# Attention scores made twice, by query and by key, in a kernel of attention and two expert layers

## The chip, the cores and the metric

The kernel runs on one core of a Trainium2 chip. The metric is the device time of one execution in microseconds (us), the median of several runs. The core has a matrix engine (TensorE, PE in the rows), a vector engine (VectorE, DVE), a scalar engine (ScalarE, ACT), GpSimd (POOL) and SyncE (SP), which issues most DMA transfers. Each engine executes its own instructions strictly in the order in which the program gave them, and waits at one whose inputs are not there.

## The reference

Cut to the first part, which the change touches; behind it stand a layer of 8 experts with balanced weights P and a two-layer network.

```python
B, H, S, D = 4, 8, 768, 64           # chunk 32, left 16, right 8, 8 memory keys
for c in range(S // 32):
    q_c = q[:, :, c_start:c_end]
    k_full = concat([mem_k, k[:, :, l_start:r_end]]); v_full = concat([mem_v, v[...]])
    scores = scale * q_c @ k_full.T
    scores = scores - max(scores)
    a = exp(scores)
    a = a / (sum(a) + 1e-9)
    out[:, :, c_start:c_end] = a @ v_full
# x: (3072, 512) -> experts: h = relu(x @ w1[e]); out += P[:, e] * (h @ w2[e]) -> relu(x @ w_in)**2 @ w_out
```

## The kernel before

Every matrix product works on pairs of fp16 numbers: a value is scaled by a power of two and split into a high part (ACT) and a low part (DVE: value minus high part), and a product is the sum of three or four products of parts.

Attention works on 32 tiles of 96 queries (three chunks) with all 8 heads, against 128 keys (16 left, 96, 8 right, 8 memory). A tile goes through `a_load` (q, k, v into a buffer `raw`), `a_scale` (maximum of q, k and v over each partition, L225, and a diagonal matrix of it, L157), `a_all` (a product with ones, L165, that brings the maxima of all partitions to each), `a_scale2` (L235 and the scale), `a_split` (high and low parts, two copies of k), `a_tqk` (q and k transposed by DMA, 24 blocks of 128 x 128), `a_scores` (a mask product L283 and 16 products L293; queries in partitions), `a_max` (L307, L309), `a_exp` (L316, 8 exponentials with the maximum as bias), `a_asplit` (high part L329, low part L330), `a_ta` (probabilities transposed by DMA, 16 blocks), `a_av` (24 products), `a_norm`, `a_xsplit` and `a_tx` (the output transposed into `xt`, 8 blocks).

Beside it runs the first expert on the tiles that are done: `gate`, `l1_pair` (24 products of 256 columns; relu on ACT, L698, low part on DVE, L699) and `l2_half` (12 products of 512 columns). Then come the balancing of the weights, the other experts and the last network, in which the change only renames banks of PSUM.

The order of the program is written out by hand. Each function gets a time on a made-up axis (`at(t, fn)`, in "units"), the list is sorted by that time and executed, so the times only set the order in which the instructions of each engine stand. Tile `i` starts at `ta(i)`, 10.957 units after the one before (`TA`); its steps lie at `OFF` behind it, for the first tiles between `TIGHT` and `OFF` (`when`). Blocks of the expert start when their tiles are done, stretched by `STR`. Steps of four or five tiles so alternate on each engine. [...]

Of the kernel before, what the change touches and what calls it, by code (L numbers as in the profile page):

```python
# [18 lines left out]
OFF = [-12.39, -1.44, 2.63, 7.14, 15.08, 26.35, 27.25, 30.29, 34.52, 41.29, 51.41, 52.02, 55.62, 62.46]  # L19
TIGHT = [-10.92, 0.2, 1.59, 2.57, 6.3, 11.37, 12.18, 16.3, 16.6, 18.11, 25.16, 25.81, 27.57, 29.09]  # L20
T0 = 5.78
TS = [6.0, 3.31, 5.8, 8.55, 10.0]
TA = 10.957
STR = 1.413
RAMP = 6.0
LDO = 4.245
SK = [0.01, 2.7, 2.52, 7.55, 7.55, 7.27, 6.55, 7.55, 7.55, 7.89, 7.55, 7.55, 5.95]
W_AT = [-4.79, 6.92, 8.93, 14.42, 18.96, 22.65, 33.67, 39.86, -4.25, 45.8, 3.81]
# [3 lines left out]
DN = [-0.34, 0.0, -0.45]  # L32
# [16 lines left out]
def tile_attention_moe_moe2(  # L49
# [14 lines left out]
    nc = tc.nc  # L64
# [23 lines left out]
    VP = 72  # L88
# [14 lines left out]
    ps = ctx.enter_context(tc.tile_pool(name="ps", bufs=3, space=bass.MemoryType.PSUM))  # L103
# [33 lines left out]
    onehot = ap_.tile([TQ, TQ], BF16, name="onehot")  # L137
    raws = [
# [83 lines left out]
    def a_scale(i):  # L222
        raw = raws[raw_of(i)]
        mx = sml.tile([P, 3], F32, tag="amx", name="amx")
        nc.vector.tensor_reduce(mx, raw, AX.X, ALU.max, apply_absolute_value=True)  # L225

        d = flat((lsb, pm)[i % 2]).bitcast(BF16).rearrange("p (n x) -> p n x", n=3)
        st[i, "dg"] = max_diag(mx, 3, d)

    def a_all(i):  # L230
        st[i, "gm"] = max_all(st.pop((i, "dg")), 3)

    def a_scale2(i):
        gm = sml.tile([P, 3], F32, tag="agm", name="agm")
        nc.vector.tensor_reduce(gm, st.pop((i, "gm")), AX.X, ALU.max)  # L235
# [13 lines left out]

    def a_split(i):  # L250
        raw = raws[raw_of(i)]
        sc = st.pop((i, "sc"))
        if i % 2 and i < LATE:
            qk = xt[NB - 1].rearrange("p s k n -> p (s k n)")[:, 0:6 * H * D]
            qk = qk.rearrange("p (a h s d) -> p a h s d", a=3, h=H, s=2)
        else:
            qk = ap_.tile([P, 3, H, 2, D], F16, tag="qk16", name="qk16")
        q16, k16 = qk[:, 0], qk[:, 1:3]
        v16 = v16s[i % NV]
        hd = lambda ap: ap.rearrange("p (h d) -> p h d", h=H)  # L260
        split(hd(raw[:, 1, :]), k16[:, 0, :, 0, :], k16[:, 0, :, 1, :], sc[:, 1:2])
        split(hd(raw[:, 0, :]), q16[:, :, 0, :], q16[:, :, 1, :], sc[:, 0:1])
        nc.vector.tensor_copy(k16[:, 1, :, 1, :], k16[:, 0, :, 0, :])
        nc.vector.tensor_copy(k16[:, 1, :, 0, :], k16[:, 0, :, 1, :])
        split(hd(raw[:, 2, :]), v16[:, 0, :, 0:D], v16[:, 1, :, 0:D], sc[:, 2:3])
        st[i, "qk"] = qk

    def a_tqk(i):
        qk = st.pop((i, "qk"))
        qkT = ap_.tile([P, 3, H, P], F16, tag="qkT", name="qkT", bufs=2)  # L270
        nc.sync.dma_start_transpose(
            out=qkT.rearrange("p a h n -> p (a h) n"), in_=qk.rearrange("p a h s d -> p (a h s d)")
        )
        st[i, "qkT"] = qkT

    def a_scores(i):
        qkT = st.pop((i, "qkT"))
        j = i % TPB
        mv = 0 if j == 0 else (2 if j == TPB - 1 else 1)
        scs = []  # L280
        for g in range(2):
            sc = psa.tile([TQ, 4, P], F32, tag="sc", name="sc", bufs=3)
# [3 lines left out]
                rhs=maskr[:, mv].unsqueeze(1).to_broadcast([TQ, 4, P]),  # L286
# [15 lines left out]

    def a_max(i):
        scs, sce = st[i, "scp"], st[i, "sce"]
        mx = sml.tile([TQ, 2, 4], F32, tag="smx", name="smx")
        for g in range(2):
            nc.vector.tensor_reduce(mx[:, g], scs[g], AX.X, ALU.max)  # L307
        nb = sml.tile([TQ, 2, 4], F32, tag="snb", name="snb")
        nc.vector.tensor_scalar(nb, mx, sce[0:TQ], -1.0, ALU.mult, ALU.mult)  # L309
        st[i, "nb"] = nb  # L310

    def a_exp(i):
        scs, sce, nb = st.pop((i, "scp")), st.pop((i, "sce")), st.pop((i, "nb"))
        e = ap_.tile([TQ, H, P], F32, tag="e", name="e")
        for h in range(H):
            nc.scalar.activation(  # L316
                e[:, h, :],
                scs[h // 4][:, h % 4, :],
                AF.Exp,
                scale=sce[0:TQ],  # L320
                bias=nb[:, h // 4, h % 4:h % 4 + 1],
            )
        st[i, "e"] = e

    def a_asplit(i):
# [1373 lines left out]
```

## Time and profile before

| | us |
|---|---|
| median of 3 runs (2658.33 to 2666.21) | 2661.05 |
| the profiled execution | 2665.82 |
| its span, first to last instruction | 2664.0 |
| busy in the span: PE, DVE, ACT, POOL | 2426.2, 1952.3, 1380.7, 1321.3 |

The span is cut in 40 slices of 66.6 us; the attention stage fills the first eight (the last transposition of its output is issued at 519.5 us). An idle engine costs time only where somebody waits for what it does next, so the views that name who waited for whom are read beside the busy times. Ends of matrix products are modelled in the trace: their starts are what can be relied on.

### The profile page before, as it was taken

Reading aid. Unit: us, or ns where it says so; the run is one execution under the profiler, and the core shown is the slowest. Engines: PE = TensorE matmul, PEld = TensorE weight load, DVE = VectorE, ACT = ScalarE, POOL = GpSimd, SP = SyncE. Lnnn points to the kernel's source line nnn. Section 1 sums busy time; section 2 is a strip of 40 time slices with the busy share of each in tenths; the row PEclk is TensorE's granted clock in tenths of the full one; section 3 lists DMA queues with packets and bytes.
Section 4 is the critical chain, followed back from the end, with each engine's and each line's share of the span. In section 5 each row is a group of like instructions: output and inputs, shape, how many; then the busy total and the mean of one; then the engine's idle time right before and its main releaser. Section 6 shows DMA issues by size and latency. Waiting matters only on the chain.

```text
span 2664.0 us, 51890 instructions
## 1 busy us (share of the span) xinstructions
PE 2426.2 (91%) x21138; PEld 2018.8 (76%) x21138; DVE 1952.3 (73%) x2844; ACT 1380.7 (52%) x2445; POOL 1321.3 (50%) x1105
## 2 busy tenths in 40 slices
PE   2578777989999999999999999999999989999998
PEld 1455545655667888888888888888888878888887
DVE  7778767476667887788787878877768897557555
ACT  4545544342334555556455555555556666666453
POOL 2211111153453566467366556655646776666343
PEclk9979978989999999999999999999999999999999
DMA  9799878423144435443534534353333365553221
GB/s 191 134 160 165 141 127 139 94 83 111 66 149 166 147 123 163 138 142 115 181 131 135 175 125 136 128 175 113 116 103 127 110 172 156 155 165 120 79 71 42
DMA packets 444471, 351.00 MB, mean 132 GB/s; under 512 B 323144, under 2 KB 377928, under 8 KB 437576
## 3 DMA queue, kind: packets, MB, share of 16 engines
q1 hardware_dynamic: 360614, 326.78, 43.3%
q10 hardware_dynamic: 83618, 20.91, 4.7%
q8 instruction: 165, 2.70, 0.4%
q14 instruction: 74, 0.61, 0.1%
HBM read 215.50 MB, written 77.07 MB: 110 GB/s over the span
## 4 chain that ended last, share of the span: by engine, by line
PE 62%; DVE 15%; POOL 4%; issue 3%; DMA 2%; ACT 2%; SPq 1%; ACTq 0%; DVEq 0%; POOLq 0%
PE pbA L822 28%; PE pbE L822 15%; PE pbB L822 7%; PE pb L822 3%; DVE xt L1020 2%; PE py L1178 2%; PE py L1180 2%; PE py L1179 2%; DVE acc L1133 1%; DVE hp L1020 1%; DVE wx L615 1%; DVE wb L615 1%; DMA w2d<-wst 1%; DVE amx L225 1%; DMA w2d<-tw 1%
## 5 line engine op out<-in xcount | busy, mean ns | idle before, releaser
L822 PEld LDWEIGHTS <-wb 128*128 128x128 f16 x5184 | 510.3, 99 | 68.4 <-DVE wb L615 4.2
L822 PEld LDWEIGHTS <-hp 128*128 128x128 f16 x4608 | 451.7, 98 | 61.8 <-issue 8.7
L822 PEld LDWEIGHTS <-wx 128*128 128x128 f16 x3888 | 380.3, 98 | 61.4 <-issue 17.6
L822 PEld LDWEIGHTS <-xt 128*128 128x128 f16 x3456 | 339.5, 99 | 81.9 <-DVE xt L1020 40.5
L822 PE MATMUL pbA<-w2p,hp 128*128 128x256 f16 x2304 | 290.7, 273 | 7.4 <-ACT xt L950 4.6
L822 PE MATMUL pbE<-xt,wx 128*128 128x256 f16 x2304 | 282.9, 273 | 14.6 <-DVE S L955 9.1
L822 PE MATMUL pbA<-S,wb 128*128 128x256 f16 x2304 | 287.4, 275 | 0.3 <-ACT S L950 0.3
L950 ACT ACTIVATE u<-pbA 128x512 f32<-128x512 f32 x181 | 107.4, 593 | 244.6 <-PE pbA L822 240.2
L330 POOL TENSOR_TENSOR a<-e,a 96x1024 f16<-96x1024 f32 x32 | 69.1, 2160 | 321.1 <-issue 204.9
L1178 PE MATMUL py<-w2p,hp 128*128 128x512 f16 x384 | 154.6, 403 | 9.4 <-DVE hp L699 5.5
L822 PE MATMUL pbA<-w2p,xt 128*128 128x256 f16 x1152 | 157.2, 273 | 0.0
L822 PE MATMUL pbE<-xt,xt 128*128 128x256 f16 x1140 | 155.5, 273 | 0.0
L822 PE MATMUL pbE<-xt,hp 128*128 128x256 f16 x1140 | 155.5, 273 | 0.0
L1179 PE MATMUL py<-w2p,hp 128*128 128x512 f16 x384 | 154.2, 401 | 0.0
L1180 PE MATMUL py<-w2p,hp 128*128 128x512 f16 x384 | 153.9, 401 | 0.0
L950 ACT ACTIVATE xt<-pbA 128x512 f32<-128x512 f32 x124 | 73.3, 592 | 140.6 <-PE pbA L822 136.0
L1020 POOL TENSOR_TENSOR hp<-u,hp 128x512 f16<-128x512 f32 x97 | 119.9, 1237 | 51.0 <-ACT hp L1013 50.3
L822 PE MATMUL pbA<-xt,wb 128*128 128x256 f16 x1152 | 142.5, 273 | 2.0 <-DVE wb L615 2.0
L822 PE MATMUL pbA<-S,wx 128*128 128x256 f16 x1152 | 141.5, 273 | 0.0
L822 PE MATMUL pbB<-xt,wb 128*128 128x256 f16 x1152 | 141.5, 273 | 0.0
L1020 DVE TENSOR_TENSOR hp<-xt,hp 128x512 f16<-128x512 f32 x80 | 88.9, 1111 | 62.1 <-ACT hp L1013 62.0
L950 ACT ACTIVATE S<-pbA 128x512 f32<-128x512 f32 x127 | 74.9, 591 | 114.2 <-PE pbA L822 112.2
(346 smaller groups left out, 5841.1 us busy)
## 6 DMA issues: line engine op xcount, KB each, us to landing
wst<-in_moe_w_dram SPq DMA_DIRECT2D x80, 512.0 KB
xt<-xdr SPq DMA_DIRECT2D x40, 1024.0 KB
S<-sdr SPq DMA_DIRECT2D x126, 256.0 KB
w2d<-wst SPq DMA_DIRECT2D x32, 512.0 KB
w2p<-w2d SPq DMA_DIRECT2D x32, 512.0 KB
wst<-in_moe_w_dram SPq DMA_DIRECT2D x56, 256.0 KB
xdr<-xt SPq DMA_DIRECT2D x12, 1024.0 KB
w2d<-tw SPq DMA_DIRECT2D x32, 384.0 KB
```

What stands on the lines that cost most here:

```text
L225: nc.vector.tensor_reduce(mx, raw, AX.X, ALU.max, apply_absolute_value=True)
L330: nc.gpsimd.tensor_tensor(al, e, ah, ALU.subtract)
L615: nc.vector.scalar_tensor_tensor(flat(d[:, 1]), f, scale(e, 0)[0], flat(d[:, 0]), ALU.mult, ALU.subtract)
L822: nc.tensor.matmul(p[:, r], lhsT=w[:, ws], rhs=x[:, xs], start=a, stop=z, skip_group_check=onto)
L950: nc.scalar.activation(t, p, AF.Copy, scale=sc)
L1020: eng.tensor_tensor(d[:, 1], t, d[:, 0], ALU.subtract)
L1133: nc.vector.scalar_tensor_tensor(a, z[:, tl], fc[:, t:t + 1], a, ALU.mult, ALU.add)
L1178: nc.tensor.matmul(p, lhsT=h[:, 1], rhs=w[:, 0], start=first, stop=False)
L1179: nc.tensor.matmul(p, lhsT=h[:, 0], rhs=w[:, 1], start=False, stop=False)
L1180: nc.tensor.matmul(p, lhsT=h[:, 0], rhs=w[:, 0], start=False, stop=last)
```

## The change

It replaces the transposition of the probabilities by a second computation of the scores. The first scores, queries in partitions, now serve the maximum alone. The maximum, split into a high and a low fp16 part (`a_max`), is transposed by a product with a unit matrix (`a_mt`, `a_mtc`); `a_st` computes the scores again with keys in partitions, and adds minus the maximum by 8 products with a constant matrix `minus` of 16 rows. So `a_exp` needs no bias per query, takes four heads in one instruction and gives probabilities that are already by key. Of the four products of parts of q and k, low times low is left out; the low parts lie in one half (64 rows) of the array, and q and k take 20 blocks of transposition.

`a_scale` no longer makes a diagonal matrix: a product with the unit matrix lays the maxima of 128 partitions in a row (`a_all`), DVE takes the row's maximum (`a_row_max`), and a product with ones spreads it (`a_spread`). High and low parts become steps of their own (`a_split`/`a_split_lo`, `a_xsplit`/`a_xsplit_lo`, `l1_pair`/`l1_lo`), a copy of q goes to POOL, and a table `STEPS` with new times replaces `OFF` and `TIGHT`; `TA` and `STR` stay. PSUM in the stage: 2 banks for `ps`, 1 for the short products, 3 for both kinds of scores, 2 for the values. `gate_prep` moves from 45.80 to 28.00 (`W_AT[9]`).

```diff
-OFF = [-12.39, -1.44, 2.63, 7.14, 15.08, 26.35, 27.25, 30.29, 34.52, 41.29, 51.41, 52.02, 55.62, 62.46]
...
+STEPS = {
+    "load": (-12.39, -10.92),
+    "mx": (-3.44, 0.20),
+    "row": (-0.44, 0.60),
+    "row_mx": (0.16, 0.90),
+    "all": (2.56, 1.20),
+    "scale": (4.56, 1.59),
+    "hi": (7.00, 2.19),
+    "lo": (8.20, 2.60),
+    "tqk": (15.08, 6.30),
+    "scores": (26.35, 11.37),
+    "max": (27.25, 12.18),
+    "mt": (30.80, 13.20),
+    "mtc": (31.00, 13.30),
+    "st": (33.80, 14.20),
+    "exp": (34.80, 15.20),
+    "ahi": (36.80, 16.20),
+    "alo": (37.00, 16.30),
+    "av": (42.00, 19.20),
+    "norm": (42.60, 19.90),
+    "xhi": (45.20, 21.70),
+    "xlo": (47.14, 21.80),
+    "tx": (53.00, 23.20),
+}
+L1LAG = 1.730
...
-    ps = ctx.enter_context(tc.tile_pool(name="ps", bufs=3, space=bass.MemoryType.PSUM))
+    ps = ctx.enter_context(tc.tile_pool(name="ps", bufs=2, space=bass.MemoryType.PSUM))
...
+    minus = ap_.tile([2 * H, H, P], F16, name="minus")
...
     def a_scale(i):
         raw = raws[raw_of(i)]
-        mx = sml.tile([P, 3], F32, tag="amx", name="amx")
+        mx = ap_.tile([P, 3], F32, tag="amx", name="amx", bufs=2)
         nc.vector.tensor_reduce(mx, raw, AX.X, ALU.max, apply_absolute_value=True)
-        d = flat((lsb, pm)[i % 2]).bitcast(BF16).rearrange("p (n x) -> p n x", n=3)
-        st[i, "dg"] = max_diag(mx, 3, d)
+        eb = ap_.tile([P, 3], I32, tag="aeb0", name="aeb0", bufs=2)
+        e16 = ap_.tile([P, 3], BF16, tag="ae16", name="ae16", bufs=2)
+        nc.vector.tensor_scalar(eb, mx.bitcast(I32), EXP_MASK, None, ALU.bitwise_and)
+        nc.vector.tensor_copy(e16, eb.bitcast(F32))
+        st[i, "e16"] = e16
     def a_all(i):
-        st[i, "gm"] = max_all(st.pop((i, "dg")), 3)
+        p = psa.tile([3, P], F32, tag="mm", name="pmax")
+        nc.tensor.matmul(p, lhsT=st.pop((i, "e16")), rhs=ident, start=True, stop=True)
+        st[i, "rows"] = p
+    def a_row_max(i):
+        p = st.pop((i, "rows"))
+        g = ap_.tile([3, 1], F32, tag="ag", name="ag", bufs=2)
+        d3 = ap_.tile([3, 3], BF16, tag="ad3", name="ad3", bufs=2)
+        nc.vector.tensor_reduce(g, p, AX.X, ALU.max)
+        nc.vector.tensor_scalar(d3, ident[0:3, 0:3], g, None, ALU.mult)
+        st[i, "d3"] = d3
+    def a_spread(i):
+        p = psa.tile([P, 3], F32, tag="mm", name="pall")
+        nc.tensor.matmul(p, lhsT=ones16[0:3, :], rhs=st.pop((i, "d3")), start=True, stop=True)
+        st[i, "gm"] = p
     def a_scale2(i):
-        gm = sml.tile([P, 3], F32, tag="agm", name="agm")
-        nc.vector.tensor_reduce(gm, st.pop((i, "gm")), AX.X, ALU.max)
+        gm = ap_.tile([P, 3], F32, tag="agm", name="agm", bufs=2)
+        nc.vector.tensor_copy(gm, st.pop((i, "gm")))
...
+    def a_split_lo(i):
+        parts, qh = st.pop((i, "parts"))
+        for src, hi, lo, scale_ in parts:
+            nc.vector.scalar_tensor_tensor(lo, src, scale_, hi, ALU.mult, ALU.subtract)
+        nc.gpsimd.tensor_copy(qh[:, :, 1, :], qh[:, :, 0, :])
...
+    def qk_of(qkT, h):
+        half = slice(64 * (h % 2), 64 * (h % 2) + 64)
+        n = H + H // 2 + h
+        return ((qkT[:, h, 0:TQ], qkT[:, n, :]), (qkT[half, H + h // 2, 0:TQ], qkT[half, n, :]))
...
+        for hh in range(4):
+            for s in range(2):
+                for u in range(2):
+                    q_, k_ = qk_of(qkT, 2 * hh + u)[s]
                     nc.tensor.matmul(
+                        scs[u][:, hh, :], lhsT=q_, rhs=k_, start=False, stop=(s == 1 and hh == 3))
...
+        nc.vector.tensor_copy(m16[:, 0], m)
+        nc.vector.tensor_tensor(m16[:, 1], m, m16[:, 0], ALU.subtract)
...
+    def a_mt(i):
+        p = psa.tile([2 * H, TQ], F32, tag="mm", name="pmt")
+        nc.tensor.matmul(
+            p, lhsT=st.pop((i, "m16")).rearrange("p s h -> p (s h)"), rhs=ident16,
+            start=True, stop=True)
+        st[i, "pmt"] = p
+    def a_mtc(i):
+        p = st.pop((i, "pmt"))
+        mt = ap_.tile([2 * H, TQ], F16, tag="mt", name="mt", bufs=2)
+        nc.scalar.activation(mt, p, AF.Copy)
+        st[i, "mt"] = mt
+    def a_st(i):
+        qkT, mt = st.pop((i, "qkT")), st.pop((i, "mt"))
+        scs = [psa.tile([P, 4, TQ], F32, tag="sc", name="sct", bufs=3) for u in range(2)]
+        for sc in scs:
+            nc.tensor.matmul(
+                sc,
+                lhsT=mask_of(i),
+                rhs=onehot.unsqueeze(1).to_broadcast([TQ, 4, TQ]),
+                start=True,
+                stop=False,
+            )
+        for u in range(2):
+            for hh in range(4):
+                nc.tensor.matmul(
+                    scs[u][:, hh, :], lhsT=minus[:, 4 * u + hh], rhs=mt, start=False, stop=False)
+        for hh in range(4):
+            for s in range(2):
+                for u in range(2):
+                    q_, k_ = qk_of(qkT, 2 * hh + u)[s]
+                    nc.tensor.matmul(
+                        scs[u][:, hh, :], lhsT=k_, rhs=q_, start=False, stop=(s == 1 and hh == 3))
...
-        for h in range(H):
-            nc.scalar.activation(
-                e[:, h, :],
-                scs[h // 4][:, h % 4, :],
-                AF.Exp,
-                scale=sce[0:TQ],
-                bias=nb[:, h // 4, h % 4:h % 4 + 1],
-            )
+        scs, sce = st.pop((i, "scp")), st.pop((i, "sce"))
+        e = ap_.tile([P, H, TQ], F32, tag="e", name="e")
+        for g in range(2):
+            nc.scalar.activation(e[:, 4 * g:4 * g + 4, :], scs[g], AF.Exp, scale=sce)
...
-    def a_ta(i):
...
-            at(0.4 * when(i, 1) + 0.6 * when(i, 2), a_all, i)
+                at(t + min(L1LAG, 2.6 * n0 / 256), l1_lo, f, b, c)
```

How the order moves is seen on three engines. DVE first, before: from the maximum over the scores of one tile (`smx`) to the maxima of another (`amx`) and their diagonal matrix, which L165 on PE waits for.

```order
L307 TENSOR_REDUCE smx<-sc 96x4 x2
L309 TENSOR_SCALAR snb<-smx,sce 96x8
L186 SCALAR_TENSOR_TENSOR qk_3257<-raw_157,asc,qk_3257 128x8x64 x2
L263 COPY qk_3257<-qk_3257 128x8x64
L264 COPY qk_3257<-qk_3257 128x8x64
L186 SCALAR_TENSOR_TENSOR v_0_158<-raw_157,asc,v_0_158 128x8x64
L364 TENSOR_SCALAR rs<-av 96x8
L365 RECIPROCAL rs<-rs 96x8
L367 TENSOR_TENSOR acc_83<-av,rs 96x512
L225 TENSOR_REDUCE amx<-acc_83 128x3
L153 TENSOR_SCALAR deb<-amx 128x3
L157 TENSOR_TENSOR pm<-ident,deb 128x384
```

The same place now; `ae` is what the row product L261 on PE takes, `ag` the row's maximum, from which comes what the spread product L274 takes.

```order
L367 TENSOR_REDUCE smx<-sc 96x4 x2
L370 CAST m_3945<-smx 96x8
L371 TENSOR_TENSOR m_3945<-smx,m_3945 96x8
L251 TENSOR_REDUCE amx<-acc_83 128x3
L254 TENSOR_SCALAR aeb_3969<-amx 128x3
L255 CAST ae_3970<-aeb_3969 128x3
L323 SCALAR_TENSOR_TENSOR qk_3962<-raw_159,asc,qk_3962 128x4x64 x2
L323 SCALAR_TENSOR_TENSOR qk_3962<-raw_159,asc,qk_3962 128x512
L323 SCALAR_TENSOR_TENSOR v_0_160<-raw_159,asc,v_0_160 128x8x64
L454 TENSOR_SCALAR rs<-av 96x8
L455 RECIPROCAL rs<-rs 96x8
L457 TENSOR_TENSOR acc_83<-av,rs 96x512
L268 TENSOR_REDUCE ag<-pmax 3x1
```

The maxima moved from behind the split and the normalisation to a place ahead of them; the row's maximum stands where they were.

PE, before: the product L165 between two blocks of the expert (`py`).

```order
L1180 LDWEIGHTS hp_95
L1180 MATMUL py<-w2p_91,hp_95 128x512
L165 LDWEIGHTS ones_97
L165 MATMUL pmax<-pm,ones_97 128x384
L1178 LDWEIGHTS hp_92
L1178 MATMUL py<-w2p_88,hp_92 128x512
```

Now, at the row product L261, with the scores by key (`sct`) right behind it.

```order
L788 LDWEIGHTS wb_86
L788 MATMUL ph_3621<-xt_74,wb_86 128x256
L261 LDWEIGHTS ae_3582
L261 MATMUL pmax<-ident,ae_3582 3x128
L393 LDWEIGHTS maskr
L393 MATMUL sct<-onehot,maskr 128x384
```

One product of 384 columns became a short one, and two masks, 8 products with `minus` and 16 of q and k follow it; the spread product L274 stands right behind these or one block of the expert later. The other places are unchanged in kind: scores, a block, (now the transposed maximum,) the values.

SP, before, one tile of each kind:

```order
L336 DMA_TRANSPOSE aT<-a_4235 128x16x96
L271 DMA_TRANSPOSE qkT<-qk_4303 128x24x128
L388 DMA_TRANSPOSE xt_76<-x_4378 128x8x96
```

Now:

```order
L329 DMA_TRANSPOSE qkT<-qk_5014 128x20x128
L481 DMA_TRANSPOSE xt_76<-x_5131 128x8x96
```

The probabilities are gone from the queue, and q and k take 20 blocks for 24.

## Rows read from the trace of the kernel before

[...]

**Rows 1.** The page, busy tenths in 40 slices of 66.6 us each.
```profile
PE   2578777989999999999999999999999989999998
PEclk9979978989999999999999999999999999999999
```

**Rows 2.** Busy time by stretch; the columns stand in the first line.
```profile
core 0: us, PE busy (x) PEld busy (x) DVE busy (x) ACT busy (x) POOL busy (x), PEclk, DMA share, GB/s
85.86:463.26 377.40, 286.99 (x2511) 199.95 (x2508) 291.09 (x554) 188.66 (x401) 68.47 (x72) 0.86 0.88 145
371.69:377.11 5.42, 5.42 (x26) 3.83 (x26) 1.24 (x2) 1.58 (x2) 2.12 (x1) 0.50 1.34 202
```

**Rows 3.** Timeline of DVE: the maximum of tile 6 and of tile 31, begin and length.
```profile
85.87 1.75 DVE L225 TENSOR_REDUCE amx<-raw 128x3 f32<-128x1536 f32 x1
...
463.26 1.74 DVE L225 TENSOR_REDUCE amx<-acc 128x3 f32<-128x1536 f32 x1
```

**Rows 4.** Waits of PE from 85.86 to 463.26 us: total, times, longest.
```profile
PE pmax L165 <- DVE lsb L157: 37.4, 12, 6.5
PE pmax L165 <- DVE pm L157: 37.4, 12, 7.9
```

**Rows 5.** Timeline of PE around one wait.
```profile
367.81 0.27 PE L696 MATMUL ph<-xt,wb 128*128 128x256 f16 x1
371.69 0.50 PE L165 MATMUL pmax<-pm,ones 128*128 128x384 bf16 x1 [3.61 <-DVE pm L157]
...
377.11 0.38 PE L283 MATMUL sc<-maskr,onehot 96*96 96x512 bf16 x1
377.33 0.61 PE L293 MATMUL sc<-qkT 128*96 128x128 f16 x8
377.78 0.38 PE L283 MATMUL sc<-maskr,onehot 96*96 96x512 bf16 x1
...
380.96 0.27 PE L696 MATMUL ph<-xt,wb 128*128 128x256 f16 x1
381.06 0.19 PE L347 MATMUL av<-v,aT 128*96 128x65 f16 x1
...
382.13 0.38 PE L1178 MATMUL py<-w2p,hp 128*128 128x512 f16 x1
```

**Rows 6.** Timeline of DVE over the same stretch.
```profile
365.67 1.41 DVE L186 SCALAR_TENSOR_TENSOR qk<-raw,asc,qk 128x512 f16<-128x512 f32 x2
367.01 0.28 DVE L263 COPY qk<-qk 128x512 f16<-128x512 f16 x1
...
369.10 1.74 DVE L225 TENSOR_REDUCE amx<-acc 128x3 f32<-128x1536 f32 x1
370.87 0.17 DVE L153 TENSOR_SCALAR deb<-amx 128x3 int32<-128x3 int32 x1
371.08 0.56 DVE L157 TENSOR_TENSOR pm<-ident,deb 128x384 bf16<-128x384 bf16 x1
```

**Rows 7.** Groups of instructions from 85.86 to 463.26 us: count, busy, mean ns, idle before.
```profile
L316 ACT ACTIVATE e<-sc,snb,sce 96x128 f32<-96x128 f32 x200 | 71.8, 455 | 3.1 <-POOL a L330 1.5 <-DVE snb L309 1.4
L307 DVE TENSOR_REDUCE smx<-sc 96x4 f32<-96x512 f32 x50 | 32.5, 679 | 15.4 <-PE sc L293 15.4
L235 DVE TENSOR_REDUCE agm<-pmax 128x3 f32<-128x384 f32 x25 | 13.7, 547 | 1.2 <-PE pmax L165 1.2
L309 DVE TENSOR_SCALAR snb<-smx,sce 96x8 f32<-96x8 f32 x25 | 6.1, 245 | 0.9
L698 ACT ACTIVATE hp<-ph 128x256 f16<-128x256 f32 x8 | 3.1, 383 | 8.0 <-PE ph L696 8.0
```

**Rows 8.** Line 293, scores: ns least, median, most; first and last start.
```profile
L293 PE MATMUL sc<-qkT x512: 217/219/342, 31.1 to 492.4; 128*96 128x128 f16 x171
```

**Rows 9.** DMA queue of SP from 85.86 to 463.26 us: packets, MB, share.
```profile
q1 hardware_dynamic: 138016, 36.50, 59.4%
```

**Rows 10.** Timeline of PE: the first gate product.
```profile
83.16 0.17 PE L398 MATMUL lgp<-g,xt 128*128 128x16 f16 x1 [6.38 <-DVE g L186]
```

More of the change, by code (lines that the diff above doesn't have):

```diff
@@ L265, in a_split @@
-        split(hd(raw[:, 2, :]), v16[:, 0, :, 0:D], v16[:, 1, :, 0:D], sc[:, 2:3])
-        st[i, "qk"] = qk
+        pair = lambda ap: ap.rearrange("p (g u d) -> p g u d", g=H // 2, u=2)
+        parts = [
+            (pair(raw[:, 1, :])[:, :, u], kk[:, :, 3 * u], kk[:, :, 1 + u], sc[:, 1:2]) for u in range(2)
+        ] + [
+            (hd(raw[:, 0, :]), qh[:, :, 0, :], ql, sc[:, 0:1]),
+            (hd(raw[:, 2, :]), v16[:, 0, :, 0:D], v16[:, 1, :, 0:D], sc[:, 2:3])]
+        for src, hi, lo, scale_ in parts:
+            nc.scalar.activation(hi, src, AF.Copy, scale=scale_)
@@ L283, in a_scores @@
+    def a_scores(i):
+        qkT = st[i, "qkT"]
+        scs = [psa.tile([TQ, 4, P], F32, tag="sc", name="sc", bufs=3) for u in range(2)]
+        for sc in scs:
             nc.tensor.matmul(
@@ L792, in s_calc, with one_bank @@
             s_split(f, a21)
+    def one_bank(nm):
+        st["third"] = (st.get("third", -1) + 1) % 3
+        if st["third"] == 2:
+            return post["psum"].tile([P, 2, Q], F32, tag="x0", name=nm, bufs=1)
+        return ps.tile([P, 2, Q], F32, tag="ps", name=nm)
     def new_bank():
@@ L940, in chain @@
             if slot == "B":
[L941 removed]
+                c[slot] = one_bank("pbB")
             else:
@@ L1322, in setup_const @@
         nc.gpsimd.memset(onehot, 0.0)
+        nc.gpsimd.memset(ident16, 0.0)
+        nc.gpsimd.affine_select(
+            out=ident16, in_=ident16, compare_op=ALU.not_equal, fill=1.0, base=0,
+            pattern=[[-1, TQ]], channel_multiplier=1)
+        nc.gpsimd.memset(minus, 0.0)
+        for part in range(2):
+            nc.gpsimd.affine_select(
+                out=minus, in_=minus, compare_op=ALU.not_equal, fill=-1.0, base=-H * part,
+                pattern=[[-1, H], [0, P]], channel_multiplier=1)
         nc.gpsimd.memset(maskr, NEG)
@@ L1340, in at @@
             ev.append((t, len(ev), fn, a))
-        fns = [
-            a_load, a_scale, a_scale2, a_split, a_tqk, a_scores, a_max, a_exp, a_asplit, a_ta,
-            a_av, a_norm, a_xsplit, a_tx,
-        ]
+        fns = {
+            "load": a_load, "mx": a_scale, "row": a_all, "row_mx": a_row_max, "all": a_spread,
+            "scale": a_scale2, "hi": a_split, "lo": a_split_lo, "tqk": a_tqk, "scores": a_scores,
+            "max": a_max, "mt": a_mt, "mtc": a_mtc, "st": a_st, "exp": a_exp, "ahi": a_asplit,
+            "alo": a_asplit_lo, "av": a_av, "norm": a_norm, "xhi": a_xsplit, "xlo": a_xsplit_lo, "tx": a_tx,
+        }
         def ta(i):
@@ L1627, in tile_attention_moe_moe2 @@
         for i in range(NA):
-            assert i < NV or when(i, 3) > when(i - NV, 10)
-            assert i < 1 or when(i, 11) > when(i - 1, 12)
+            assert i < NV or when(i, "hi") > when(i - NV, "av")
+            assert i < 1 or when(i, "all") > when(i - 1, "scale") and when(i, "row") > when(i - 1, "row_mx")
+            assert i < 1 or when(i, "mt") > when(i - 1, "mtc") and when(i, "exp") > when(i - 1, "alo")
+            assert i < 1 or when(i, "norm") > when(i - 1, "xlo")
         for n in range(4):
```

134 lines of the change are left out of this document (60 added, 74 removed).

## The prediction

> **What bounds the kernel now.** The page's slices come first [rows 1]: from slice 8 on (533 us) PE is at 9 of 10 and its clock at 9. Before that, in the attention stage, PE stands at 7 or 8 and its granted clock dips to 7 or 8. The change touches that stage alone, so what is decided there decides the time. The window table gives the steady part, from the maximum of tile 6 to that of tile 31 [rows 2, 3]: 377.4 us for 25 tiles, 15.1 us a tile. PE was busy 287.0 us of it, so 90.4 us idle, at a mean clock of 0.86. DVE was busy 291.1 us, 11.6 a tile; ACT 7.5, POOL 2.7; the DMA engines 0.88 of the time.
>
> The waits of PE say who is late: 74.8 us of the 90.4, in 24 of the 25 tiles, stand before one product, L165, which sums the maxima of the next tile, and every one ends with DVE's L157 [rows 4]. The timelines show a whole one. PE ends its last product near 368.0 and starts L165 at 371.69 [rows 5]; meanwhile DVE works without a gap through split, copies, normalisation, the maximum L225 at 369.10 and L157 at 371.08 [rows 6]. From the split to the end of L157 it is 6.0 us, with the maximum over the scores (2 x 0.68 for L307 and 0.25 for L309, [rows 7]) 7.6 us between "scores are there" and "L165 may go". PE has less than that to do in between. [...] A mean clock of 0.86 means some 28% of the stretch at the lower level, 106 us; work there loses at most half, 53 us; since part of that time is idle anyway I take 40.
>
> **The change, part by part**, for the 25 tiles of that stretch.
>
> 1. PE, added: scores by key, per tile 2 mask products of 384 columns, 8 that add minus the maximum, 16 of q and k. A mask product of 512 columns takes 0.22 us from start to start (377.11 to 377.33), the 8 score products 0.45 us, 0.056 each, and the 24 of a tile's values 1.07 us (381.06 to 382.13), 0.045 each [rows 5]. So 2 x 0.165 and 24 x 0.05: 1.5 us. Three short products (row, spread, transposed maximum, about 0.05 each) replace L165 of 384 columns (0.165): nothing. Sum 25 x 1.5 = 37 us, all on PE and not hidden.
> 2. PE, unknown: 23 times a tile the height or width of a product changes, since the low parts of q and k now fill 64 rows of the array, the minus products 16 rows, two short ones few columns. Nothing of this is in the trace, where all products are 96 or 128 rows high. Upper end: a product lasts 0.219 us [rows 8] while its successor starts after 0.056; if each change of shape lets nothing overlap, it costs 0.163 us, 23 x 0.163 = 3.7 us a tile, 94 us. Lower end: the 8 pairs of half-height products a tile run side by side, a gain of 8 x 0.056 = 0.45 us, 11 us. The nearest rows are changes of operand: from 256 columns to 65 (380.96 to 381.06) and from 65 to 512 at 382.13 no product starts late [rows 5]. I therefore take a value near the low end, 0.04 us each: 0.9 us a tile, 23 us.
> 3. DVE: L157 (0.56), two copies (0.28 each) and L309 (0.25) go, L235 (0.55) shrinks to a copy of 3 columns [rows 6, 7]. Added: seven small steps, at the 0.17 us of a small step (L153 at 370.87): cast, maximum of a row of 128, product 3x3, copy, two steps for the maximum in two halves, and one more split instruction: 1.2 us. Net 0.7 us less of 11.6. The low part of the hidden layer is issued 1.73 units after its product and no longer right behind it, so DVE finds it ready more often; I count nothing for it.
> 4. DVE, order: this is what I think counts. The maximum over the tile moves ahead of the split's low parts and of the normalisation, so after the scores DVE does 1.36 + 0.35 + 1.74 + 0.35 = 3.8 us, and not 7.6, until PE's row product may go. PE has 1.07 us of values and one or two blocks of 24 products (2.6 us each) in between: covered. In its place stand two new waits. The spread product needs the row's maximum, which on DVE stands behind low parts and normalisation, another 3.8 us; PE has 1.5 us of scores by key and no or one block of 2.6: 0 to 2.3 us late, 1.0 in the mean. The transposed maximum needs, after the spread product, scale and maximum on DVE (four small steps, 1.36, 0.35 and a step of 0.7 or two: some 3.5 us) against scores and a block, 3.9: 0.4 with jitter. So I put PE's idle time at 1.45 us a tile, 36 us in place of 90: 54 us less. Gaps that short do not resemble the 3.9 us after which the clock fell; I leave 8 of the 40 us of slow clock: 32 less.
> 5. ACT: 8 exponentials a tile of 0.455 us [rows 7] become 2 of 384 columns (0.38 at 256 columns, [rows 7], so 0.5 each): 2.6 us less. ACT was busy half the time, and none of PE's long waits ends with it: nothing. But its steps also free the banks of the expert's products, and there are 2 of these now, not 3 shared with L165; the other bank's block, 2.6 us, covers ACT's step (0.38 us at half the columns, [rows 7]) and DVE's like one. If it didn't, PE would stand up to a step a block, 3 blocks a tile.
> 6. SP and DMA: per tile 48 blocks of transposition become 28 (16 of the probabilities go, 4 of q and k). SP's queue took 59.4% of the DMA engines [rows 9]; the share falls by 59.4 x 20/48 = 25 points. DMA was not what PE waited for, so nothing for that, but the two hand-offs of the probabilities through SP go, and loads land sooner. The new load is issued later, 6.3 units of the order table ahead of its maximum and not 9.1; with a free DMA that holds.
> 7. POOL: one copy more a tile; at 2.7 us of 15 a tile it is hidden; were it late, the transposition of q and k behind it would be, which has 11 units of the table until the scores.
> 8. Start: PE stood 6.4 us before its first gate product, waiting for DVE's split of the gate weights [rows 10], which moves from unit 45.8 to 28.0 of the table: 6 us less. After the stage nothing changes but the names of PSUM banks.
>
> Sum: +37 +23 -54 -32 -6 = **-32 us**. The profiled execution took 2665.8 us, 4.8 above the median of the three runs; it would be at 2634, the median at 2661 - 32 = **2629 us**.
>
> [...] The trace has no product of less than 96 rows. [...]
>
> **Rivals.** A, *each change of shape empties PE*: 23 x 0.163 us a tile, 94 us in place of 23, so +71; PE would then be late itself and wait less (-20): about -32 + 71 - 20 = +19, **2680 us**. For it: a product outlasts its distance fourfold [rows 8]. Against: changes of operand cost nothing [rows 5]. It decides from 0.163 down to about 0.09 us a change, where 23 x 25 x (0.09 - 0.04) = 29 us eat the forecast. B, *the wait moves*: DVE still has 10.9 us a tile in strict order, with three meeting points with PE in a tile and not one; if idle time and slow clock stay at 90 and 40 us, the 60 us of added products stand bare: -6 + 60, **2715 us**; with half of the relief, 2672. For it: the DVE chain of points 3 and 4 is as long as PE's work. C, *both unknowns fall well*: changes cost nothing, pairs run side by side, half of the remaining waits vanish: -32 - 23 - 11 - 18 = -84, **2577 us**. D, *it does not do what it says*: the probabilities' transposition is gone from the SP queue in the order of the change, so only its worth is open.
>
> **How the numbers follow.** 0.3% of this kernel is 8 us, about what a measurement can tell from no change. Forecast (2600 to 2650): 0.5, nearly all faster. C (below 2600): 0.15, faster. A: 0.15, of it a third within 8 us and two thirds slower. B: 0.2, of it 0.05 still faster, 0.05 the same, 0.1 slower. Faster 0.68, same 0.11, slower 0.21. The range leaves out the far ends of A, B and C: 2588 to 2672; the forecast's own is 2600 to 2650.
>
> **What would show it.** Right: mean distance of the tile maximum near 14 us; no wait of 3 us before the row product; clock 0.95 or more in the stage; DMA at 5 or 6 of 10. A shows in the starts of the half-height products: 0.05 us after the one before, or 0.2. B shows in PE's waits at the spread product or the transposed maximum, above 3 us a tile. Wrong altogether: a stage that ends no earlier than 520 us, or a difference after 560 us.

## The result and the profile after

The changed kernel takes 2690.3 us (2683.3 to 2695.9, 4 runs); the kernel before, on the same chip, 2662.6. The ratio is 1.0103, 95% interval 1.0075 to 1.0132: slower by 1%, where 2629 us and a range up to 2672 were forecast. The profiled execution took 2690.8 us, its span 2689.0. The page's slices, as [rows 1] (PEclk is the granted clock, there in tenths of full speed and by stretch as a share of it; a row of a timeline begins with its start and its length in us):

```profile
PE   2899999988999999999999999999999989899998
PEclk9889999999999999999999999999999999999999
DMA  7466755231335333534443434444333365563221
```

PE is now at 9 of 10 through most of the attention stage (the first eight slices), and the DMA engines are at 4 to 7. Both were wanted, and the time rose: PE is busy for longer than the added products need. The steady part, from the maximum of tile 6 to that of tile 31 (timeline of DVE, then busy time by stretch with the columns of [rows 2], as in all such lines below):

```profile
95.06 1.74 DVE L251 TENSOR_REDUCE amx<-raw 128x3 f32<-128x1536 f32 x1
...
478.15 1.75 DVE L251 TENSOR_REDUCE amx<-acc 128x3 f32<-128x1536 f32 x1
```

```profile
95.10:478.10 383.00, 355.20 (x3198) 236.23 (x3197) 248.49 (x601) 150.53 (x299) 71.98 (x97) 0.93 0.63 109
```

Against [rows 2] PE's idle time went from 90.4 to 27.8 us and the clock from 0.86 to 0.93, close to the forecast; but PE's busy time rose by 68 us, at the better clock. The stretch is 5.6 us longer, where 26 less were forecast. PE's waits in it, as [rows 4] (total, times, longest):

```profile
PE sc L347 <- ACT e L416: 8.5, 7, 3.6
PE lgp L491 <- ACT lg L505: 4.3, 8, 0.6
PE ph L786 <- DVE hp L795: 3.0, 1, 3.0
PE pmt L377 <- DVE m L371: 2.1, 2, 1.8
...
PE pmax L261 <- DVE qk L323: 1.5, 1, 1.5
PE pmax L261 <- DVE xt L323: 1.5, 1, 1.5
PE pmt L377 <- DVE agm L279: 1.2, 1, 1.2
PE pmax L261 <- DVE rs L454: 1.1, 1, 1.1
PE pmax L261 <- DVE ae L255: 1.0, 2, 0.6
...
PE pall L274 <- DVE ad L269: 0.6, 1, 0.6
```

The 75 us before the product of the next tile's maxima are gone, and nothing of that size stands in their place: rival B is out as the main cause. What PE does, the timeline shows for one tile:

```profile
304.05 1.75 PE L358 MATMUL sc<-qkT 128*96 128x128 f16 x16
305.74 0.39 PE L1281 MATMUL py<-w2p,hp 128*128 128x512 f16 x1
...
312.92 0.50 PE L393 MATMUL sct<-onehot,maskr 96*128 96x384 bf16 x2
313.35 0.51 PE L402 MATMUL sct<-mt,minus 16*128 16x96 f16 x8
313.79 1.43 PE L408 MATMUL sct<-qkT 128*128 128x96 f16 x16
315.22 0.16 PE L274 MATMUL pall<-ad,ones 3*128 3x3 bf16 x1
```

The 16 products of scores need 1.69 us until the next block may start, where a product of this size took 0.056 us before [rows 5], 0.90 for 16. The single starts say where. Below, from the same trace and from those of three experiments, stands the distance in ns from the start of each of the 16 to the next start (median over the tiles that ran at full clock). F is a product of full height (128 rows of the array), h one of half (64); the sets by query and by key are the first and the second scores:

```
                    order F F h h, four times
changed, by query   59 147 3 183  93 149 3 183  93 149 3 183  93 149 3 186   sum 1679
changed, by key     53 138 3 145  53 138 3 145  53 138 3 145  53 138 3 145   sum 1356
                    e1_group: F eight times, then h eight times
by query            59  55 55 55  56  56 56 149  3  90 4  52   3  53 3 149   sum  898
by key              53  43 43 42  42  42 43 138  3  50 3  39   3  39 3 135   sum  721
                    e4_many: F h, eight times
by query           149 183 187 183 187 183 187 183 187 183 187 183 187 183 187 186  sum 2925
by key             149 146 148 146 149 145 149 146 148 146 149 145 149 146 148 146  sum 2355
                    e11_pad_full: F sixteen times
by query            59  55 55 55  56  56 56  56 56  56 56  56  56  56 56  56  sum  896
by key              43  43 42 43  42  42 42  43 42  43 42  42  42  42 42  43  sum  680
```

Two half-height products cost about one place, as hoped; but each step from one height to the other makes a start 0.09 to 0.13 us late, and the first full product after such a step can have a late successor too (by query 93 ns in place of 59). e1_group has six changes fewer in a set, so the sums price one: (1679 - 898)/6 = 130 ns by query, (1356 - 721)/6 = 106 by key; 0.12 us in the mean, where point 2 took 0.04. This is the sign that the prediction named for rival A.

The loads of the weights show where the time goes. Among the products of both sets of scores in the changed kernel's steady part (medians), where two of full height follow each other the load for the second starts 40 ns (by query) or 11 ns (by key) after the first product and 54 or 42 ns ahead of its own; at a change of shape it starts 134 to 182 ns after the product before, and its own product follows 2 to 4 ns behind. So at a change the next weights are not loaded ahead. Why not, these runs don't show.

In the order of PE's products the shape changes 735 times, 23 a tile, if 96 and 128 rows or columns count as one shape (the kernel before has no other).

### The profile page after: what moved, and what is told of

Same layout as the page of the kernel before. It is cut to its first block, busy times and chain, and to the rows that moved or that the text cites. A ratio compares the mean times of both kernels' runs of the same rounds, so it can differ in the third digit from the quotient of the medians.

```text
span 2689.0 us, 53589 instructions
## 1 busy us (share of the span) xinstructions
PE 2520.6 (94%) x22034; PEld 2066.8 (77%) x22034; DVE 1911.4 (71%) x2908; ACT 1330.4 (49%) x2317; POOL 1327.7 (49%) x1142
## 4 chain that ended last, share of the span: by engine, by line
PE 72%; DVE 15%; POOL 4%; issue 3%; ACT 2%; DMA 2%; SPq 1%; ACTq 0%; DVEq 0%; POOLq 0%
PE pbA L925 27%; PE pbE L925 15%; PE pbB L925 7%; PE pb L925 3%; PE py L1281 3%; PE py L1282 3%; PE py L1283 3%; DVE xt L1123 2%; PE sc L358 2%; PE sct L408 2%; PE ph L786 2%; PE ph L788 1%; PE ph L787 1%; DVE acc L1236 1%; DVE hp L1123 1%
## 5 line engine op out<-in xcount | busy, mean ns | idle before, releaser
L428 POOL TENSOR_TENSOR aT<-e,aT 128x768 f16<-128x768 f32 x32 | 52.4, 1639 | 299.4 <-ACT aT L422 261.9
L1281 PE MATMUL py<-w2p,hp 128*128 128x512 f16 x384 | 150.1, 391 | 7.0 <-DVE hp L795 3.7
L1282 PE MATMUL py<-w2p,hp 128*128 128x512 f16 x384 | 150.0, 391 | 0.0
L1283 PE MATMUL py<-w2p,hp 128*128 128x512 f16 x384 | 149.3, 389 | 0.0
```

Source lines behind the costliest of these rows:

```text
L428: nc.gpsimd.tensor_tensor(aT[:, 1], st.pop((i, "e")), aT[:, 0], ALU.subtract)
L1281: nc.tensor.matmul(p, lhsT=h[:, 1], rhs=w[:, 0], start=first, stop=False)
L1282: nc.tensor.matmul(p, lhsT=h[:, 0], rhs=w[:, 1], start=False, stop=False)
L1283: nc.tensor.matmul(p, lhsT=h[:, 0], rhs=w[:, 0], start=False, stop=last)
```

## The experiments

Theory T: the changes of shape cost the time. Rivals: the added products themselves (N), a wait that takes PE's place once it is relieved (W), and for the start of the kernel the gate's early split (G) or the order of the loads (O). A fourth, that PE is slow to add to the same sums again after only one other product, falls with e11_pad_full below, which keeps that order. The expectations price a change at 0.092 us, the lateness of one start; the sums above came with the runs. All kernels were measured against the kernel before (2661 to 2663 us) on their chip; the last three columns are of the steady part.

| kernel | median us | ratio, 95% interval | changes of shape | length | PE busy | clock |
|---|---|---|---|---|---|---|
| changed | 2690.3 | 1.0103 (1.0075 to 1.0132) | 735 | 383.0 | 355.2 | 0.93 |
| e1_group | 2649.4 | 0.9955 (0.9940 to 0.9971) | 351 | 351.9 | 316.7 | 0.94 |
| e2_pad | 2672.9 | 1.0048 (1.0033 to 1.0063) | 512 | 368.3 | 335.1 | 0.94 |
| e3_group_pad | 2642.0 | 0.9931 (0.9908 to 0.9953) | 128 | 344.8 | 297.5 | 0.95 |
| e4_many | 2787.5 | 1.0489 (1.0458 to 1.0520) | 1247 | 466.4 | 445.7 | 0.86 |
| e11_pad_full | 2651.5 | 0.9957 (0.9941 to 0.9974) | 0 | 348.6 | 296.2 | 0.96 |
| e5_pad_serial | 2645.5 | 0.9935 (0.9921 to 0.9950) | 128 | 349.7 | 302.0 | 0.93 |
| e12_no_bykey | 2631.6 | 0.9884 (0.9866 to 0.9902) | 64 | 344.7 | 290.9 | 0.93 |

**Products in groups (e1_group).** In both sets:

```diff
-        for hh in range(4):
-            for s in range(2):
+        for s in range(2):
+            for hh in range(4):
                 for u in range(2):
```

> The 16 products of q and k of each of the two sets of a tile are issued as eight full-height ones and then eight half-height ones: 351 changes of shape in the program in place of 735, the same products. Theory T (each change costs PE the 0.092 us that the starts of the changed kernel show, and PE is the bound of the steady part): 384 x 0.092 = 35 us less than the changed kernel's 2690, 2655, a little below the kernel before (2662); the product after a run of full ones still starts some 0.09 us late, but once a set and not four times. Rival N (the loss is the added products themselves and the start, changes of shape are overlapped): 2690 within 8. Rival W (PE gets shorter but a wait for DVE or ACT takes its place): 2675 to 2690, with PE's idle time of the steady part up from 1.1 to 2 us a tile or more.

41 us less than the changed kernel, where T asked for 35, by the order of the 16 products in each set alone; it is now faster than the kernel before. PE's busy time in the steady part fell by 38.5 us for 300 changes, 0.128 each; its idle time rose by only 7.4. N and W fall as main causes.

**Short products filled up (e2_pad), and both (e3_group_pad).**

```diff
-    minus = ap_.tile([2 * H, H, P], F16, name="minus")
+    minus = ap_.tile([P, H, P], F16, name="minus")
...
-        d3 = ap_.tile([3, 3], BF16, tag="ad3", name="ad3", bufs=2)
+        d3 = ap_.tile([P, 3], BF16, tag="ad3", name="ad3", bufs=2)
...
-        p = psa.tile([2 * H, TQ], F32, tag="mm", name="pmt")
+        p = psa.tile([P, TQ], F32, tag="mm", name="pmt")
...
```

> The short products (maxima of a tile, their spread, the transposed maximum, the eight with minus) are filled up with zeros to 128 rows and columns, so that they have the shape of all others: 512 changes in place of 735, all between full and half height. T: 223 x 0.092 = 21 us less than 2690, 2669. N: 2690 within 8; if weights of 128 columns in place of 3 or 16 cost anything, slower by at most 96 x 0.06 = 6 us.

> Both edits: 128 changes of shape in place of 735. T: 607 x 0.092 = 56 us less than 2690, 2634, faster than the kernel before (2662) by some 28, which is about what the prediction promised (2629 with a price of 0.04 for 23 changes a tile). W: 2655 to 2680, because DVE (11 us a tile) ends the waits once PE is short of 13 us a tile. N: 2690 within 8.

17 and 48 us less, of the 21 and 56 that T asked for; more zeros, less time. Busy time by stretch, PE's waits and its timeline in the kernel with both (`e` of line 257 is here the padded operand of the row product):

```profile
92.45:437.20 344.75, 297.54 (x3202) 217.02 (x3200) 254.34 (x602) 149.54 (x299) 71.33 (x97) 0.95 0.74 121
```

```profile
PE sc L349 <- ACT e L417: 12.1, 8, 3.7
PE pmax L263 <- DVE e L257: 8.7, 8, 4.4
PE pmax L263 <- ACT mt L386: 5.0, 3, 2.9
```

```profile
300.78 0.97 PE L360 MATMUL sc<-qkT 128*96 128x128 f16 x16
301.68 0.28 PE L787 MATMUL ph<-xt,wb 128*128 128x256 f16 x1
...
316.08 0.78 PE L409 MATMUL sct<-qkT 128*128 128x96 f16 x16
```

The 16 scores need 0.90 us in place of 1.69. PE's busy time is 57.7 us less for 475 changes (0.121 each), the stretch 38 less: the other 19 came back as waits for ACT and DVE (idle 27.8 to 47.2 us), so W holds for a third of it.

**More changes (e4_many).**

```diff
         for hh in range(4):
-            for s in range(2):
-                for u in range(2):
+            for u in range(2):
+                for s in range(2):
```

> The same products in the order full, half, full, half: no two half-height products stand side by side, 1247 changes of shape in place of 735. T: 512 x 0.092 = 47 us more than 2690, and 256 pairs that no longer run side by side, 0.05 each, 13 more: 2737 to 2750. N: 2690 to 2703. If the cost of a change were hidden under the product before: 2703.

97 us more, well above T. The starts account for (2925 + 2355 - 1679 - 1356) ns = 2.25 us a tile, 72 us in 32. The rest goes with a lower clock: 0.86 in the mean, though PE is busy 96% of the stretch. Behind the line of the steady part, three short stretches show it:

```profile
99.40:565.80 466.40, 445.74 (x3197) 285.13 (x3197) 249.10 (x602) 153.20 (x302) 72.64 (x98) 0.86 0.51 90
316.30:320.00 3.70, 3.70 (x27) 1.80 (x26) 1.82 (x4) 0.53 (x2) 0.00 (x0) 1.00 0.00 0
320.00:323.10 3.10, 3.10 (x39) 2.12 (x36) 1.91 (x6) 0.82 (x3) 0.00 (x0) 1.00 0.79 157
323.10:329.90 6.80, 6.79 (x40) 4.63 (x40) 0.23 (x1) 1.22 (x3) 0.00 (x0) 0.50 1.11 153
```

From 316.3 to 329.9 the records show PE without a gap, and yet its clock was 0.50 from 323.1, in the middle of the 16 products by key that change shape at every step:

```profile
321.72 2.74 PE L408 MATMUL sct<-qkT 128*128 128x96 f16 x16
324.39 0.40 PE L786 MATMUL ph<-xt,wb 128*128 128x256 f16 x1
```

So it is mostly in e4_many: 21 of the 25 falls of the clock in its steady part come after 2.9 to 46 us without a gap in PE's records. In the kernel before and in the changed kernel each fall in that part comes in a gap or shortly behind one, at most 0.8 and 2.1 us. Only the order of the products differs from the changed kernel and from e1_group, so the order brings it; by what way isn't shown. A product's end is modelled, so "without a gap" says only that the next start came before that end.

**No change of shape at all (e11_pad_full):** e2_pad with 24 blocks of q and k again, as before the change. This also gives POOL a second copy a tile.

```diff
-    NQK = 2 * H + H // 2
+    NQK = 3 * H
...
-        return ((qkT[:, h, 0:TQ], qkT[:, n, :]), (qkT[half, H + h // 2, 0:TQ], qkT[half, n, :]))
+        return ((qkT[:, h, 0:TQ], qkT[:, H + h, :]), (qkT[:, h, 0:TQ], qkT[:, 2 * H + h, :]))
```

> The 20 blocks of q and k are undone: 24 blocks, all products of full height, as before the change (each block of q against two blocks of k), on top of the filled-up short products. No change of shape is left in the program (0 of 735; 512 in the run that only filled up the short products, 2673). T: 512 changes less at 0.092 to 0.12, 47 to 61 us, and 256 side-by-side pairs become products of 0.056 of their own, 14 more: 2626 to 2640, PE's starts 0.055 apart through both sets of scores. N: 2673 within 8. If the DMA's four blocks more a tile matter (its share of the steady part goes back from 0.66 to about 0.75) PE waits for transposed q and k: above 2645.

21 us less than e2_pad, 12 short of T's range. PE's busy time did fall as T has it (335.1 to 296.2); half of it came back as waits:

```profile
PE sc L345 <- ACT e L413: 12.2, 8, 3.4
PE pmax L263 <- DVE e L257: 9.4, 7, 3.7
PE pall L276 <- DVE ad L271: 6.1, 7, 2.6
```

PE has no wait for the transposed q and k among the larger ones, so the four blocks more do not hold PE directly. Its 296.2 us are 9 more than before the change, those of the changed kernel 68 more: 59 of the 68 go with the shapes, the lower clock included. With the half-height products grouped (e3_group_pad) PE is busy for as long as with none: what the pairs save, the four changes a tile take. That e3_group_pad is 9 us faster is not explained by PE; its interval touches that of e11_pad_full. Whether the blocks or POOL's copies (98.7 us busy, 72.4 in e2_pad) delay ACT and DVE stays open.

**Neighbours in the same half (e5_pad_serial):** e3_group_pad with the loops in the order s, u, hh.

> The kernel with both edits to the shapes (2642), with the eight half-height products of a set in another order: the four of the upper half, then the four of the lower half, so that no two neighbours lie in different halves but one pair. Shapes change as often (128). If neighbours in different halves really run side by side (0.003 us apart in the records, against 0.055), six of eight pairs a tile are lost, 6 x 0.055 = 0.33 us, 32 tiles: 11 us more, 2653; with a part of it hidden in PE's waits 2646 to 2653. If the 0.003 is only how the records are written and the pair costs two places anyway: 2642 within 4.

Not told apart from 2642.0. Products of the same half came in pairs too, 13 ns apart and not 3, and the 16 by query needed 905 ns, not 896. So the small distance is no proof of two halves at work at once: a half-height product costs half a place whichever half its neighbour has, and why, these runs don't show. Going from one half to the other cost nothing; the lost 0.12 us belongs to changes of height.

**Without the products by key (e12_no_bykey):** e3_group_pad without the 16 of line 409, which leaves the scores out of the probabilities.

> The kernel with both edits to the shapes (2642), with the 16 products of q and k by key left out (the by-key scores then hold only the mask and minus the maximum, so the probabilities are not those of the reference). This takes 0.71 us a tile from PE (starts of the 16 at full clock), 23 us over 32 tiles. If PE's work still sets the pace there: 2619. If below some 300 us of PE work in the steady part the waits for DVE and ACT set it: those waits grow by what PE is relieved of, PE's idle time of the steady part rises from 47 to some 60 us, and the time is 2632 to 2640. Between: 2619 to 2632, by the share of the removed work that comes back as waits.

10 of the 23 us came out, none in the steady part: 344.7 us as with them. Of the 17.8 us of products taken out there PE's busy time fell by 6.6 only, since the clock was lower (0.93 for 0.95), and its idle time rose to 53.7. At 0.71 us a tile the scores by key are cheap and mostly covered; they are not what made the kernel slower.

**The start.** The changed kernel reaches the maximum of tile 6 at 95.06 us, the kernel before at 85.87 [rows 3]. The timelines of POOL and ACT there:

```profile
55.23 2.13 POOL L659 TENSOR_TENSOR wb<-acc,wb 128x1024 f16<-128x1024 f32 x1 [1.46 <-ACT wb L658]
62.98 0.41 POOL L516 PARTITION_ALL_REDUCE gall<-gmx  x1 [5.63 <-issue]
```

```profile
54.11 1.04 ACT L658 ACTIVATE wb<-acc 128x1024 f16<-128x1024 f32 x1
63.99 0.32 ACT L211 ACTIVATE g<-graw,gsc 128x32 f16<-128x32 f32 x1 [8.84 <-DVE gsc L205]
64.22 0.22 ACT L385 ACTIVATE mt<-pmt 16x96 f16<-16x96 f32 x1
```

The maximum of the gate weights is taken over the partitions by an all-reduce on POOL, which stands 5.6 us before it begins. The wait is 5.71 us in the kernel before and in e3_group_pad and 5.81 in e9_before_early_gate, whether DVE's maximum came 0.7 us into it (76.44 us in the kernel before) or 3.1 us into it (60.48 in the changed kernel), so it is not a wait for that; what it is, these runs don't show. ACT waits 8.8 us for what follows from it, with the transposed maximum behind. Four kernels move or replace it. The edit

```diff
-W_AT = [-5.06, 6.92, 8.47, 14.42, 18.96, 22.65, 33.67, 39.86, -3.33, 28.00, 3.81]
+W_AT = [-5.06, 6.92, 8.47, 14.42, 18.96, 22.65, 33.67, 39.86, -3.33, 44.00, 3.81]
```

stands on top of e3_group_pad in e6_late_gate and alone in e8_after_late_gate;

```diff
-W_AT = [-4.79, 6.92, 8.93, 14.42, 18.96, 22.65, 33.67, 39.86, -4.25, 45.8, 3.81]
+W_AT = [-4.79, 6.92, 8.93, 14.42, 18.96, 22.65, 33.67, 39.86, -4.25, 28.00, 3.81]
```

is the kernel before with the early split (e9_before_early_gate), and

```diff
-        nc.gpsimd.partition_all_reduce(gall, gmx, channels=P, reduce_op=RED.absmax)
+        wsc["g"] = max_diag(gmx, 1, sml.tile([P, 1, P], BF16, tag="dg", name="dg", bufs=1))
...
+        at(W_AT[9] + 1.0, weight_all, "g")
+        at(W_AT[9] + 2.0, gate_split)
```

takes that maximum on PE and DVE, on top of e3_group_pad (e7_pe_gate).

> The kernel with both edits to the shapes (2642), with one more: the gate weights' maximum and split stand at 44.0 units of the order table in place of 28.0, just ahead of the first gate product, as they stood before. Theory G (moving them forward cost time: ACT stands 8.9 us before the gate's split because POOL's all-reduce takes 5.7 us to begin, behind it wait the transposed maximum of tile 2, the by-key scores, the buffer of transposed q and k, and the scores of tile 3): the maximum of tile 5 comes at 72 in place of 79.0, that of tile 6 at 86 to 89 in place of 92.5; of these 4 to 7 us PE loses up to 5 again before the first gate product: 2636 to 2642. The prediction's own sign (the move forward is worth 6): 2648. Rival O (the start is late for the order of the loads and nothing else): maxima of tiles 5 and 6 unchanged within 1 us.

> The kernel with both edits to the shapes (2642), with the gate weights' maximum at 28.0 as there, but taken over the partitions by a product on PE and a maximum on DVE, as the other weights' is, and not by POOL's all-reduce. G: no wait of 8.9 us on ACT at the gate's split, no hole of 13 us on POOL from 56 to 69; the maximum of tile 5 at 72, of tile 6 at 86 to 88, and no wait before the first gate product: 2633 to 2637. O: maxima of tiles 5 and 6 unchanged within 1 us, 2642 within 4.

> The changed kernel (2690) with nothing else but the gate weights' maximum and split at 44.0 in place of 28.0. G: the maximum of tile 5 at 73 in place of 80.3, that of tile 6 at 88 to 91 in place of 95.1; 2684 to 2690. The prediction's point 8 (the move is worth 6 us): 2696. O: both maxima unchanged within 1 us, 2690 to 2696.

> The kernel before (2661) with the gate weights' maximum and split at 28.0 in place of 45.8 and nothing else. Prediction's point 8: the 6.4 us that PE stands before its first gate product go, 6 less, 2655. G: there too ACT waits for POOL's all-reduce, now among the first tiles; the gain is eaten, 2658 to 2666, and the maxima of tiles 4 to 6 come 3 to 8 us later.

e9_before_early_gate: 2675.2 us, ratio 1.0047 (1.0029 to 1.0064), 12.6 us slower than the kernel before where point 8 said 6 faster and G had 2658 to 2666; ACT waits 10.5 us at the gate's split, and the maximum of tile 6 comes 8.4 us later, while the steady part is as long as before (377.4). ACT's wait, POOL's timeline and DVE's maximum:

```profile
ACT g L185 <- DVE gsc L179: 10.5, 1, 10.5
```

```profile
51.76 4.79 POOL L567 TENSOR_TENSOR wb<-acc,wb 128x1024 f16<-128x1024 f32 x2
62.35 0.41 POOL L423 PARTITION_ALL_REDUCE gall<-gmx  x1 [5.81 <-issue]
69.98 2.11 POOL L567 TENSOR_TENSOR wb<-acc,wb 128x1024 f16<-128x1024 f32 x1 [7.22 <-issue]
```

```profile
94.29 1.75 DVE L225 TENSOR_REDUCE amx<-raw 128x3 f32<-128x1536 f32 x1
```

In the new order the place matters little: 2694.6 us (e8; 1.0120, 1.0097 to 1.0143) and 2641.7 (e6; 0.9926, 0.9908 to 0.9945) with the split late again, neither told apart from 2690.3 and 2642.0. What the early tiles gain (tile 5 at 76.1 in place of 80.3 in e8) the first gate product loses (96.9 in place of 93.2), and tile 6 comes 4 to 5 us later in both, where G had it some 4 to 6 earlier: wherever the all-reduce stood in these runs, somebody waited. With the maximum on PE (e7) both gain, tile 6 stands at 86.52 in place of 92.45, and still the median is 2641.7 (0.9926, 0.9902 to 0.9950): expectation missed. The profiled execution, the fastest of the four at 2636.3, is 5.9 us shorter than that of e3_group_pad; the other three took 2640.5 to 2648.0, so the 6 us are shown for the start and not for the time.

**The order of the first loads (e10_pe_gate_loads).** Not in the prediction at all: the change moves the expert's first weights from -4.79 to -5.06 of the order table, and tile 0's loads from 5.78 - 10.92 = -5.14 to 6.11 - 10.92 = -4.81, so the weights now go first through SP's queue. SP's timeline, and DVE's first maximum of a tile, in the changed kernel:

```profile
0.72 5.24 SPq L590 DMA_DIRECT2D acc<-in_moe_w_dram  x8
6.01 0.61 SPq L226 DMA_DIRECT2D raw<-in_k_dram  x1
```

```profile
16.21 1.75 DVE L251 TENSOR_REDUCE amx<-raw 128x3 f32<-128x1536 f32 x1 [5.02 <-DMA raw<-in_q_dram]
```

```diff
-W_AT = [-5.06, 6.92, 8.47, 14.42, 18.96, 22.65, 33.67, 39.86, -3.33, 28.00, 3.81]
+W_AT = [-4.60, 6.92, 8.47, 14.42, 18.96, 22.65, 33.67, 39.86, -3.33, 28.00, 3.81]
```

This is e7_pe_gate with the weights behind tile 0 again.

> The kernel with both edits to the shapes and the gate's maximum on PE (2642), with the first loads of the expert's weights issued after those of tile 0 again (unit -4.60 in place of -5.06), as before the change. If that order is what delays the first tile: its maximum at 13.3 us in place of 15.5, tile 6 at 84 in place of 86.5, and 2 to 3 us less, 2639; DVE's wait of 5 us for the last load of tile 0 gone. If not: maxima of tiles 0 and 6 within 1 us of 15.5 and 86.5.

2636.1 us, ratio 0.9897 (0.9882 to 0.9912), the lowest of all kernels here that compute the whole result, 27 us below the kernel before. Tiles 0 and 6 come when they were expected to:

```profile
13.28 1.74 DVE L253 TENSOR_REDUCE amx<-raw 128x3 f32<-128x1536 f32 x1
...
84.35 1.74 DVE L253 TENSOR_REDUCE amx<-raw 128x3 f32<-128x1536 f32 x1
```

The starts are shown; the medians of e7 and e10 are not told apart, and part of the gain is lost behind tile 6 (349.4 us to tile 31, in place of 347.4 in e7 and 344.8 in e3_group_pad).

## Why the prediction was wrong

By its own sum the profiled span should have been 2632; it was 2689.0, 57 us more. Of these 31.6 lie in the steady part (383.0 against 351.4), 15.2 ahead of it (95.1 us against 85.9 - 6: the 6 that did not come, and 9.2 more), 11.2 between the last maximum and the last product of the first expert's first layer (95.9 against 84.7 us), and -1.1 behind. Taking 607 changes of shape away gives back 48. The start comes back in steps: tile 6 stands at 92.45 us without those changes, at 86.52 with the gate's maximum on PE as well, at 84.35 with the old order of the loads.

- **Point 2 failed**, and with it the forecast: "The nearest rows are changes of operand ... I therefore take a value near the low end, 0.04 us each." A change of operand is not like a change of shape. The runs show 0.12 us a change, three times the value and near the upper end (0.163): 23 x 25 x 0.12 = 69 us of PE time in the steady part and not 23. This is rival A, above its own point of decision (0.09); its 2680 lies 10 below the result. A step to another height cost 0.12 us, a step to the other half at the same height nothing that e3_group_pad and e5_pad_serial show (the starts of a pair lie 3 ns apart across the halves and 13 within one). That PE empties, as A has it, is not seen in the records themselves.
- **Point 1 right**: with the shapes grouped the set by key takes, for the 8 minus and 16 score products, 8 x 0.042 + 0.71 = 1.05 us, and its two masks 0.33: 1.4 us, 1.5 forecast.
- **Point 4 right that the long wait goes, and near its 36 us of idle time by luck**: 27.8 us were measured, but PE's slowness hid part; relieved, it is 47 to 52. Nor does it stand where it was put: before the spread product 0.6 us (25 forecast) and the transposed maximum 3.3 (10), but 8.5 at the banks of the scores, 5.1 at the row product and 4.3 at the gate. The clock recovered to 0.93, 53 us of the stretch at the lower level (0.50, as in the second line of [rows 2]) in place of 106, which by the prediction's own working is 20 us less and not 32.
- **Points 3, 5, 6, 7 right**: DVE fell to 9.9 us a tile (10.9 forecast), ACT, POOL and DMA end no long wait in the steady part but ACT's 8.5 us at the banks of the scores; SP's queue took 36.2% of the DMA engines there (34 forecast).
- **Point 8 failed**, in the old order even in sign. The split moved forward was costed by the 6.4 us it saves at the gate [rows 10], and not by the all-reduce that moves with it and the queue of ACT behind; in the old order the move costs 12.6 us, in the new one it brings nothing that can be measured. The order of the loads, worth 2.2 us at tile 0 and tile 6 (e7 against e10), was not seen in the two numbers that show it.
- **After the stage nothing differs**, as forecast. In the tail the tiles under way still carry their added products: of the 11.2 us there 7 go with the shapes (88.7 us in e3_group_pad).

## What to carry to other kernels

Before a product is made smaller, count how often PE's order goes from one height or width to another, and price each at the 0.12 us of these runs rather than by the rows of changes of operand; issue like shapes together, or fill short operands with zeros, whose cost does not show here. When an engine is relieved, look for the wait that is second: of 58 us taken from PE 38 came out. A step that is moved forward takes along what it issues on every other engine, and those queues may be late in its new place (12.6 us in e9_before_early_gate).

## What was not expected of the hardware

- Half-height products cost half a place each in e1_group and e5_pad_serial (in one shape, two start 0.003 to 0.013 us apart and the next 0.03 to 0.05 later), whether neighbours lie in different halves or in one.
- The clock can fall without a gap in PE's records: in e4_many, where the height changes at each of the 32 products of scores, PE stood at 0.50 in stretches that no gap precedes, and the mean clock of the steady part was 0.86 at 96% busy.
- POOL's all-reduce of one column leaves that engine without other work for 13 us in e9_before_early_gate (56.6 to 70.0), 0.41 of them busy: 5.8 ahead of it and 7.2 behind, in both of which it waits for nothing that the profile shows. In the kernel before, with the call at 81.5, it is 5.7 and 7.3. (The length of such an instruction is rough in the trace.)
